# Turning score blocks three groups ahead instead of two, and mixing token groups in pairs, in a fused gated-attention and token-mixing kernel

## The chip, the cores and the metric

The kernel runs on one core of a Trainium2 chip. The metric is device time in microseconds (us); lower is better. Engines are called as in the profile: PE is TensorE's matmul side and PEld its weight load, DVE is VectorE, ACT is ScalarE, POOL is GpSimd, SP is SyncE, which here only issues transfers. A name with a q at its end (SPq, POOLq) is the engine's sequencer.

## The reference, cut to what matters

```python
# B, S, D = 8, 3200, 256; d_qk = d_hyper = 64; inputs and output are float32
scores = (1.0 / S) * np.matmul(z, z.transpose(0, 2, 1))     # symmetric: token by token
attn   = np.maximum(scores, 0.0) ** 2
x      = u * np.matmul(attn, v)
wq, wk = x @ w_q, x @ w_k
W_tok  = (1.0 / np.sqrt(64)) * np.einsum('bsd,btd->bst', wq, wk)
mixed  = np.einsum('bst,btd->bsd', W_tok, x)
out    = np.maximum(mixed, 0.0) @ w_out
```

Nothing in `W_tok` is nonlinear, so the kernel never makes it. It forms the 64 x 256 matrix "heads" = wk^T x of a batch, and then mixes: mixed = wq times heads.

## The kernel before, in words

**Tiling.** The 3200 tokens of a batch are 25 tiles of 128, taken in seven groups: six of 512 tokens and a last one (`LASTG`, group 6) of 128. A score tile is 128 key tokens by the 512 queries of one group. The attention matrix is symmetric, so a block that was computed for groups (gi, gj), gi < gj, can serve (gj, gi) when it is transposed. `is_turned` (L177) says for which pairs that is done: gj at most `FAR` = 2 groups further, or gj the last group. The transposing is a DMA from SP (L268) from the tile `at` to `tt1`, `tt2` (by the distance) or `ttl`, and `weights` (L272) picks the direct or the turned block. The profile calls all numbered buffers `tt`.

**Phases.** The text is one long loop, `while groups` (L601); every pass is called a phase here, counted by `k`. A phase scores six new tiles as three pairs (four tiles, when it also mixes), L211: the two matmuls of a pair use 64 rows each and lie in the two halves of the array. DVE or ACT takes a pair out of PSUM (`first_stage`, L230/L234, tile `g`), and one phase later POOL or ACT squares it (`second_stage`, L247/L249, tile `at`). Two phases after its scoring (`LAG`), a tile may be used by the second product (L289), 128x256 matmuls into `acc`; each group needs 25 tiles times four column blocks (25 times one for group 6). The loop spreads a group over `m` phases by when its own tiles will have been scored; rows that come from turned blocks fill up (`left`).

**After a group's last phase,** `gate` (L315) multiplies by `u` on DVE into `x_sb`, and SP turns it (L327). Phases later `keys_and_heads` projects it (L337; `wqk` gives 64 rows of q and 64 of k), ACT writes it to `qk` (L348, pool `pq` with nine buffers), SP turns that to `kx` (L353). When the next group is keyed, `double_keys_queries` copies q to the other 64 partitions by a DMA (L361) and the keys to the other half of `kx` on POOL (L362), so that `heads` (L368) comes out doubled; DVE adds it up (L381) and closes it into `hs` (L387). `mix` (L416) then does one group, both halves of the model width side by side, `mix_out` applies relu on ACT (L428), and `proj` (L441) with `proj_out` (L463/L468/L469) makes and stores the output. One `mix` and its `proj` share a phase.

**The transfers' order.** SP issues everything that is not a load of `v` or `z` in the order of the text, and waits in that order: a transpose whose `at` is not squared yet holds the load of `u` behind it. POOL issues the loads of `v` (L127) and `z` (L131) between its squarings. `group_begun` (L555) sets the phases in which loads are due: `load_u` of the next group one phase after a group has begun.

**The end.** After the loop the keys of the last group are not turned but replaced by a Gram matrix (`last_gram`, `last_heads`); what is left of batch 6 and all of batch 7 is mixed, projected and stored there.

Of the kernel before, what the change touches and what calls it, by code (L numbers as in the profile page):

```python
# [16 lines left out]
def kernel(  # L17
# [25 lines left out]
    FAR = 2  # L43
# [6 lines left out]
    NAT = 14  # L50
# [9 lines left out]
    pg = ctx.enter_context(tc.tile_pool(name="pg", bufs=8))  # L60
# [4 lines left out]
    pq = ctx.enter_context(tc.tile_pool(name="pq", bufs=9))  # L65
    prt = ctx.enter_context(tc.tile_pool(name="prt", bufs=3))
# [82 lines left out]
    wq32 = consts.tile([P, ND, dh], FP32, tag="wq32", name="wq32")  # L149
    wk32 = consts.tile([P, ND, dh], FP32, tag="wk32", name="wk32")  # L150
    wqk = consts.tile([P, ND, 2, dh], FP16, tag="wqk", name="wqk")
    wq2 = consts.tile([P, ND, 2, dh], FP16, tag="wq2", name="wq2")
    wk2 = consts.tile([P, ND, 2, dh], FP32, tag="wk2", name="wk2")
    wo = consts.tile([P, ND, D], FP16, tag="wo", name="wo")
    wo32 = {}

    def load_weights():
        wo32[0] = px.tile([P, ND, D], FP32, tag="x_sb", name="wo32")
        nc.sync.dma_start(out=wq32[:], in_=moe_w_q.rearrange("(c p) h -> p c h", p=P))
        nc.sync.dma_start(out=wk32[:], in_=moe_w_k.rearrange("(c p) h -> p c h", p=P))  # L160
        nc.sync.dma_start(out=wo32[0][:], in_=moe_w_out.rearrange("(c p) e -> p c e", p=P))

    def cast_weights():
        nc.gpsimd.tensor_copy(out=wqk[:, :, 0, :], in_=wq32[:])
        nc.gpsimd.tensor_copy(out=wqk[:, :, 1, :], in_=wk32[:])
        for half in range(2):
            nc.gpsimd.tensor_copy(out=wq2[:, :, half, :], in_=wq32[:])
            nc.gpsimd.tensor_copy(out=wk2[:, :, half, :], in_=wk32[:])
        nc.gpsimd.tensor_copy(out=wo[:], in_=wo32[0][:])
# [7 lines left out]
    def is_turned(gi, gj):  # L177
        return gi < gj and (gj <= gi + FAR or gj == LASTG)

# [7 lines left out]
    for b in range(B):  # L187
        for gi in range(NG):
            near = [t for t in range(NT) if is_turned(gi, group_of(t))]
            own = [  # L190
                t for t in range(NT) if t not in near and not is_turned(group_of(t), gi)
            ]
# [47 lines left out]
    def second_stage(p0, g, on_act):  # L240
        at = pat.tile([P, 2 * W], FP16, tag="at", name="at")
        at0 = 0
        for hs, w in pieces(p0):
            n = hs.stop - hs.start
            out = at[:, at0 : at0 + n * w].rearrange("p (n w) -> p n w", w=w)
            if on_act:
                nc.scalar.square(out=out, in_=g[:, hs, 0:w])  # L247
            else:
                nc.gpsimd.tensor_mul(out=out, in0=g[:, hs, 0:w], in1=g[:, hs, 0:w])  # L249
            at0 += n * w  # L250
        at0, blocks = 0, []
        for tile_ in tiles[p0 : p0 + 2]:
            b, gi, ti = tile_
            made[tile_] = (at, at0)
            gj = group_of(ti)
            if is_turned(gi, gj):
                blocks.append((b, gi, gj, ti - starts[gj] // P, 1, at0, at0 + widths[gi]))
            at0 += widths[gi]
        if len(blocks) == 2 and blocks[0][:3] == blocks[1][:3] and blocks[1][3] == blocks[0][3] + 1:
            blocks = [blocks[0][:4] + (2, blocks[0][5], blocks[1][6])]  # L260
        for b, gi, gj, n0, nn, c0, c1 in blocks:
            if (b, gi, gj) not in turned:
                kind, nr, bufs = ("l", 1, 8) if gj == LASTG else (gj - gi, 4, gj - gi + 2)
                turned[b, gi, gj] = ptt.tile(
                    [P, nr, 4, P], FP16, tag=f"tt{kind}", name=f"tt{kind}", bufs=bufs
                )
            out = turned[b, gi, gj][:].rearrange("p n j t -> p (n j) t")
            nc.sync.dma_start_transpose(out=out[:, 4 * n0 : 4 * (n0 + nn), :], in_=at[:, c0:c1])  # L268
# [55 lines left out]
    def turn_x(b, gi):  # L324
        nn = widths[gi] // P
        xTs[b, gi] = pxt.tile([P, 4, ND, P], FP16, tag="xT_sb", name="xT_sb")
# [18 lines left out]
    def projections_out(b, gi, out):  # L345
        gw = widths[gi]
        qks[b, gi] = pq.tile([P, W], FP16, tag="qk", name="qk")
        nc.scalar.copy(out=qks[b, gi][:, 0:gw], in_=out)  # L348

    def turn_keys(b, gi):  # L350
        gw = widths[gi]
        ks[b, gi] = pk.tile([P, 4, 2, dh], FP16, tag="kx", name="kx")
        nc.sync.dma_start_transpose(  # L353
            out=ks[b, gi][:, 0 : gw // P, :, :].rearrange("p n a h -> p n (a h)"),
# [3 lines left out]
    def double_keys_queries(b, gi):  # L358
        gw = widths[gi]
        nn = gw // P  # L360
        nc.sync.dma_start(out=qks[b, gi][dh:P, 0:gw], in_=qks[b, gi][0:dh, 0:gw])  # L361
        nc.gpsimd.tensor_copy(out=ks[b, gi][:, 0:nn, 0, :], in_=ks[b, gi][:, 0:nn, 1, :])  # L362

    def heads(b, gis, ps, stop=True):

        parts = [(gi, n) for gi in gis for n in range(widths[gi] // P)]
        for gi, n in parts:
            nc.tensor.matmul(  # L368
                out=ps[:, 1, 0:D],
                lhsT=ks[b, gi][:, n, :, :].rearrange("p a h -> p (a h)"),  # L370
# [5 lines left out]
    def heads_out(b, gis, ps):  # L376
        if gis[0] == 0:
            hacc[b] = psml.tile([P, D], FP32, tag="ha", name="ha")
            nc.vector.tensor_copy(out=hacc[b][:], in_=ps[:, 1, 0:D])
        elif gis[-1] < LASTG:  # L380
            nc.vector.tensor_add(out=hacc[b][:], in0=hacc[b][:], in1=ps[:, 1, 0:D])  # L381
        else:
            heads_done(b, ps[:, 1, 0:D])

    def heads_done(b, part):
        hss[b] = psml.tile([P, D], FP16, tag="hs", name="hs")
        nc.vector.tensor_add(out=hss[b][:], in0=hacc.pop(b)[:], in1=part)  # L387
# [13 lines left out]
    def last_heads(b, g32, ps):  # L401
        for cc in range(ND):
            nc.tensor.matmul(
                out=ps[:, 1, 0:D],
                lhsT=wk2[:, cc, :, :].rearrange("p t h -> p (t h)"),
                rhs=g32[:, ds(cc * D, D)],
                start=False,
# [3 lines left out]
    def mix(b, gi):  # L411
        gw = widths[gi]
        ps = ps_tile("mx")
        for db in range(ND):
            half = db * dh
            nc.tensor.matmul(  # L416
                out=ps[:, db, 0:gw],
                lhsT=hss[b][half : half + dh, ds(db * P, P)],
                rhs=qks[b, gi][half : half + dh, 0:gw],
# [5 lines left out]
    def mix_out(b, gi, ps):  # L425
        gw = widths[gi]
        rts[b, gi] = prt.tile([P, ND, W], FP16, tag="rt", name="rt")
        nc.scalar.activation(out=rts[b, gi][:, :, 0:gw], in_=ps[:, :, 0:gw], func=RELU)  # L428
# [50 lines left out]
    def side_mix(b, ps):  # L479
        for db in range(ND):  # L480
            nc.tensor.matmul(
                out=ps[:, 1, ds(D + db * P, P)],
                lhsT=hss[b][:, ds(db * P, P)],
# [5 lines left out]
    def side_mix_out(b, ps):  # L489
# [3 lines left out]
            func=RELU, scale=0.5,  # L493
# [19 lines left out]
    todo_mix, todo_between, at_phase, side = [], [], {}, []  # L513
# [14 lines left out]
    def keys_and_heads(b, gis):  # L528
# [3 lines left out]
        projections(b, gis[0], wqk, outs[0])  # L532
        aside = None
        if keyed:
            heads(*keyed[0], ps, stop=(len(gis) == 1 and not side))
            if len(gis) > 1:
                projections(b, gis[1], wqk, outs[1], start=False)
# [6 lines left out]
        if keyed:  # L544
            hb, hgis = keyed.pop(0)
            heads_out(hb, hgis, ps)
            if hgis[-1] == LASTG:
                todo_mix.extend((hb, i) for i in range(LASTG))
# [6 lines left out]
    def group_begun(k, b, gi):  # L555
# [4 lines left out]
        if gi == 0 and b + 1 < B:  # L560
# [4 lines left out]
            for i in range(5):  # L565
                due(k + later + 5 + 3 * i, lambda i=i: load_v(b + 1, 5 * i, 5))
# [19 lines left out]
    def mix_due(k):  # L586
        if len(groups) > NG:
            return todo_mix and k - mixed_at[0] >= 3
        return len(todo_mix) > 2 and k - mixed_at[0] >= 2 and not key_due(k)
# [11 lines left out]
    while groups:  # L601
# [5 lines left out]
        if mix_due(k):  # L607
            mb, mg = todo_mix.pop(0)
            mixed_at[0] = k
            mixing = (mb, mg, mix(mb, mg))  # L610
# [8 lines left out]
        if keying and keyed:  # L619
            for g_ in keyed[0][1]:  # L620
                double_keys_queries(keyed[0][0], g_)
        if mixing:
            mix_out(*mixing)
        staged = []
# [29 lines left out]
        if begins:  # L654
# [5 lines left out]
            if m == 4 and need > produced + (4 if mix_due(k + 1) else 6):  # L660
# [20 lines left out]
        if mixing:  # L681
            mb, mg, _ = mixing
# [3 lines left out]
        elif keying:  # L686
            extra = todo_between.pop(0)[1]
        cut = 10 if extra else 0
# [28 lines left out]
    for g_ in hgis:  # L717
        double_keys_queries(hb, g_)
    psh = ps_tile("hd")
    heads(hb, hgis, psh, stop=False)  # L720
# [4 lines left out]
    for mb, mg in todo_mix[:2]:  # L725
        mix_out(mb, mg, mix(mb, mg))
    last_heads(last, g32, psh)
    heads_done(last, psh[:, 1, 0:D])
    for mb, mg in todo_mix[2:]:
        mix_out(mb, mg, mix(mb, mg))  # L730
# [4 lines left out]
    for i, (mb, mg) in enumerate(todo_mix):  # L735
        if i == 0:
            store(mb, mg, [acc_tile(0, "fo0")[:], acc_tile(1, "fo1")[:]],
                  [(True, nc.sync, 2), (True, nc.sync, 2)])
        else:
            store(mb, mg)  # L740
    qs = [(LASTG - 1, ps_tile("qq")[:, 0, :]), (LASTG, acc_tile(0, "qq")[:, 0:P])]
    for gi, o in qs:
        projections(last, gi, wq2, o)
    for gi, o in qs:
        projections_out(last, gi, o)
    mix_out(last, 0, mix(last, 0))
    for gi in range(LASTG - 1):
        mix_out(last, gi + 1, mix(last, gi + 1))
        if gi == LASTG - 2:
            mix_out(last, LASTG, mix(last, LASTG))  # L750
        store(last, gi)
# [32 lines left out]
```

## Time and profile before

| what | value |
|---|---|
| median of 3 runs | 808.53 us (808.15 to 812.89) |
| the profiled execution: time, span | 807.18 us, 805.4 us |
| PE, PEld busy, share of the span | 98%, 73% |
| DVE, ACT, POOL busy | 61%, 59%, 60% |
| score matmuls (L211), matmuls into `acc` (L289) | 920, 5000 |
| transposes of score blocks issued by SP (`tt`, `ttl`) | 146, 48 |
| mean traffic of the DMA engines | 178 GB/s |

The span goes from the first to the last instruction of the program; 1.8 us of the execution's time lie around it. A group line of the profile reads: line, engine, operation, tile written <- tiles read, shapes, count | busy us, mean ns of one | idle time of the engine before it, and what ended it. The DMA share is the time of all packets over that of 16 engines.

### The profile page before, as it was taken

What the parts mean: (1) busy time and instruction counts of PE and PEld (TensorE: products, weight loads), DVE (VectorE), ACT (ScalarE), POOL (GpSimd) and SP (SyncE); (2) the same over time, 40 slices, a digit from 0 to 9 for tenths busy, and PEclk for the clock granted to TensorE, in tenths of its full rate; (3) what the DMA queues carried; (4) which work ended last, traced back from release to release, by engine and by line L of the source; (5) the groups of instructions that cost most, each with busy time, mean ns of one, the idle gap of its engine ahead of it and who ended that gap; (6) DMA issues with size and microseconds to landing.
All of it is one profiled execution on the core that took longest, in us unless ns stands there. A gap on an engine that the chain in (4) does not pass through costs nothing.

```text
span 805.4 us, 16696 instructions
## 1 busy us (share of the span) xinstructions
PE 788.8 (98%) x6778; PEld 584.9 (73%) x6778; DVE 493.1 (61%) x514; ACT 475.1 (59%) x526; POOL 485.2 (60%) x352
## 2 busy tenths in 40 slices
PE   7999999999999999999999999999999999999996
PEld 4777777777777777777777777777777767767774
DVE  5766666565665566755676556765666656655525
ACT  6655556556765556565675556656665565565534
POOL 7957676564666557755666466864676555655420
PEclk9999999999999999999999999999999999999999
DMA  7999899997989969998899979999999996867436
GB/s 175 149 198 192 141 176 181 212 190 134 216 148 208 200 152 194 176 208 186 175 157 211 198 157 178 188 206 175 184 197 157 182 217 143 159 148 183 116 98 246
DMA packets 330878, 143.20 MB, mean 178 GB/s; under 512 B 307441, under 2 KB 313137, under 8 KB 330801
## 3 DMA queue, kind: packets, MB, share of 16 engines
q1 hardware_dynamic: 302528, 125.90, 76.4%
q0 software_dynamic: 28128, 15.98, 17.7%
q8 instruction: 53, 0.87, 0.5%
q10 hardware_dynamic: 144, 0.26, 0.1%
q14 instruction: 25, 0.20, 0.1%
HBM read 59.38 MB, written 26.21 MB: 106 GB/s over the span
## 4 chain that ended last, share of the span: by engine, by line
PE 95%; issue 1%; POOL 1%; DMA 1%; DVE 1%; ACT 0%; SPq 0%; POOLq 0%; DVEq 0%
PE acc L289 69%; PE sc L211 13%; PE fo L441 5%; PE qk L368 3%; PE qk L337 3%; PE mx L416 2%; POOL at L249 1%; DMA z<-in_z_dram 1%; DMA xT_sb<-x_sb 0%; DVE x_sb L315 0%; DVE fo L463 0%; PE qk L499 0%; ACT qk L348 0%; SPq L95 0%; DVE g L234 0%
## 5 line engine op out<-in xcount | busy, mean ns | idle before, releaser
L249 POOL TENSOR_TENSOR at<-g 128x1024 f16<-128x1024 f32 (+2 forms) x234 | 430.3, 1853 | 222.2 <-DVE g L234 136.8
L234 DVE TENSOR_SCALAR g<-sc 128x1024 f32<-128x1024 f32 (+1 forms) x340 | 388.1, 1184 | 188.5 <-PE sc L211 188.1
L289 PE MATMUL acc<-v_sb,at 128*128 128x256 f16 x3656 | 446.8, 273 | 0.4 <-DVE x_sb L315 0.4
L289 PEld LDWEIGHTS <-at 128*128 128x128 f16 x3656 | 344.7, 98 | 108.0 <-issue 66.6
L230 ACT ACTIVATE g<-sc 128x1024 f32<-128x1024 f32 x128 | 131.2, 1025 | 199.6 <-PE sc L211 199.6
L247 ACT ACTIVATE at<-g 128x1024 f16<-128x1024 f32 (+2 forms) x234 | 236.9, 1029 | 0.6 <-DVE g L234 0.6
L289 PE MATMUL acc<-v_sb,tt 128*128 128x256 f16 x1152 | 149.1, 273 | 0.0
L211 PE MATMUL sc<-zT 64*128 64x512 f16 x920 | 129.7, 381 | 2.3 <-DVE hs L387 0.9
L289 PEld LDWEIGHTS <-tt 128*128 128x128 f16 x1152 | 112.5, 98 | 12.9
L315 DVE TENSOR_TENSOR x_sb<-acc,u_sb 128x512 f16<-128x512 f32 (+1 forms) x104 | 69.3, 668 | 66.8 <-PE acc L289 62.5
L428 ACT ACTIVATE rt<-mx 128x1024 f16<-128x1024 f32 (+1 forms) x49 | 49.1, 1012 | 56.8 <-PE mx L416 55.3
L211 PEld LDWEIGHTS <-zT 64*128 64x128 f16 x920 | 34.9, 95 | 50.1 <-issue 28.5
L362 POOL COPY kx<-kx 128x256 f16<-128x256 f16 (+1 forms) x54 | 20.1, 378 | 65.9 <-DMA kx<-qk 65.7
L468 ACT ACTIVATE fo<-fo 128x1024 f32<-128x1024 f32 (+1 forms) x40 | 40.6, 1014 | 24.4 <-PE fo L441 22.6
L441 PE MATMUL fo<-wo,rt 128*128 128x256 f16 x386 | 49.6, 273 | 1.7 <-DVE fo L463 0.9
L348 ACT CAST qk<-qk 128x512 f16<-128x512 f32 (+1 forms) x54 | 28.7, 545 | 27.5 <-PE qk L368 13.2
L441 PEld LDWEIGHTS <-rt 128*128 128x128 f16 x386 | 37.2, 98 | 7.5 <-ACT rt L428 1.9
L381 DVE TENSOR_TENSOR ha<-ha,qk 128x256 f32<-128x256 f32 x31 | 13.1, 421 | 30.0 <-ACT qk L348 30.0
L368 PE MATMUL qk<-x_sb,kx 128*128 128x256 f16 x191 | 28.4, 273 | 1.9 <-POOL kx L362 1.9
L337 PE MATMUL qk<-xT_sb,wqk 128*128 128x512 f16 (+1 forms) x108 | 29.9, 358 | 0.0
L368 PEld LDWEIGHTS <-kx 128*128 128x128 f16 x195 | 19.0, 98 | 14.2 <-POOL kx L362 2.4
L289 PE MATMUL acc<-v_sb,ttl 128*128 128x256 f16 x192 | 22.6, 273 | 0.0
(47 smaller groups left out, 150.2 us busy)
## 6 DMA issues: line engine op xcount, KB each, us to landing
u_sb<-in_u_dram SPq DMA_DIRECT2D x48, 512.0 KB, 4.8
out_dram<-fo SPq DMA_DIRECT2D x46, 512.0 KB, 4.2
v_sb<-in_v_dram POOLq DMA_DIRECT2D x35, 320.0 KB, 5.7
qk<-qk SPq DMA_DIRECT2D x47, 64.0 KB, 4.0
zd<-in_z_dram POOLq DMA_DIRECT2D x7, 400.0 KB, 8.1
tt<-at SPq DMA_TRANSPOSE x146, 4.3
u_sb<-in_u_dram SPq DMA_DIRECT2D x8, 128.0 KB, 3.0
xT_sb<-x_sb SPq DMA_TRANSPOSE x56, 4.1
```

What stands on the lines that cost most here:

```text
L211: nc.tensor.matmul(out=sc[:, h, 0:gw], lhsT=zT[b][half : half + dqk, ts(ti, P)], rhs=zT[b][half : half + dqk, ds(gs, gw)], start=True, sto ...
L230: nc.scalar.activation(out=g[:, hs, 0:w], in_=sc[:, hs, 0:w], func=RELU, scale=GSCALE)
L234: nc.vector.tensor_scalar(out=g[:, hs, 0:w], in0=sc[:, hs, 0:w], scalar1=0.0, scalar2=GSCALE, op0=AOP.max, op1=AOP.mult,)
L247: nc.scalar.square(out=out, in_=g[:, hs, 0:w])
L249: nc.gpsimd.tensor_mul(out=out, in0=g[:, hs, 0:w], in1=g[:, hs, 0:w])
L289: nc.tensor.matmul(out=accs[j // 2][:, ds((j % 2) * D, D)], lhsT=weights(b, gi, ti, j), rhs=vs[b][:, ti, :], start=(first and ti == rows_[ ...
L315: nc.vector.tensor_mul(out=xs[b, gi][:, 2 * half : 2 * half + n, :].rearrange("p n d -> p (n d)"), in0=accs[half][:, 0 : n * D], in1=us[b, ...
L337: nc.tensor.matmul(out=out, lhsT=w[:, ac, :, :].rearrange("p t h -> p (t h)"), rhs=xTs[b, gi][:, 0 : gw // P, ac, :], start=(start and ac ...
L368: nc.tensor.matmul(out=ps[:, 1, 0:D], lhsT=ks[b, gi][:, n, :, :].rearrange("p a h -> p (a h)"), rhs=xs[b, gi][:, n, :], start=((gi, n) == ...
L428: nc.scalar.activation(out=rts[b, gi][:, :, 0:gw], in_=ps[:, :, 0:gw], func=RELU)
L441: nc.tensor.matmul(out=banks[jf // 2][:, ds((j - jf) * D, D)], lhsT=rt[:, dc, ts(j, P)], rhs=wo[:, dc, :], start=(dc == 0 and j == jf), st ...
L468: nc.scalar.mul(out=flat_out[:, sl], in_=part, mul=FINAL_SCALE)
```

## The change

- **Turned blocks.** `is_turned` takes the batch too: three groups further for batches 0 to 6, two for the last. Buffers: three for each of the distances 1, 2 and 3 (distance 2 had four), seven for the last group (eight before).
- **Order of a group's tiles.** Rows that are turned for the next group come first, and the single tile 24 goes to the end or the start, so that pairs stay whole.
- **q of odd groups on the other half.** A second weight tile `wkq` has k first and q second. Odd groups and group 6 are projected with it. The DMA copy of q (L361) and the POOL copy of the keys (L362) are gone; `heads` keeps only the half that holds k^T x, even and odd groups apart, and `heads_crossed` adds the two halves once per batch.
- **Mixing in pairs.** One `mix` does two groups for one half of the model width, with one matmul in each half of the array; the projections of the two groups wait in a list `todo_proj` until both halves are mixed, and take one phase each.
- **Group 6** has small tiles of its own for turned x and for q; its side mix uses `hz`, whose first 64 rows are zero.
- **Pools.** `at` 13 (14), `g` 7 (8), `qk` 11 (9), `rt` 2 of double size (3).
- **Loads.** `load_v` starts two phases earlier in a batch (four in the first one).
- **The end.** Two half mixes of batch 6 and two of its projections are left for the end (before: three mixes and three projections); batch 7 is mixed in pairs there too, and one relu of its first pair goes to DVE.

```diff
-    def is_turned(gi, gj):
-        return gi < gj and (gj <= gi + FAR or gj == LASTG)
+    def is_turned(b, gi, gj):
+        far = 3 if b + 1 < B else 2
+        return gi < gj and (gj <= gi + far or gj == LASTG)
...
-            elif len(tiles) % 2:
-                order = own[:1] + near + own[1:]
             else:
-                order = near + own
+                single = [NT - 1]
+                order = [t for t in near if group_of(t) == gi + 1 < LASTG]
+                order += [t for t in own + near if t not in order + single]
+                order = single + order if len(tiles) % 2 else order + single
...
-                kind, nr, bufs = ("l", 1, 8) if gj == LASTG else (gj - gi, 4, gj - gi + 2)
+                kind, nr, bufs = ("l", 1, 7) if gj == LASTG else (gj - gi, 4, 3)
...
-    def double_keys_queries(b, gi):
-        gw = widths[gi]
-        nn = gw // P
-        nc.sync.dma_start(out=qks[b, gi][dh:P, 0:gw], in_=qks[b, gi][0:dh, 0:gw])
-        nc.gpsimd.tensor_copy(out=ks[b, gi][:, 0:nn, 0, :], in_=ks[b, gi][:, 0:nn, 1, :])
+    def swapped(gi):
+        return gi % 2 == 1 or gi == LASTG
...
     def heads_out(b, gis, ps):
+        mine = slice(0, dh) if swapped(gis[0]) else slice(dh, P)
...
+        acc, part = hacc[b][mine, :], ps[mine, 1, 0:D]
+        if gis[0] < 2:
+            nc.vector.tensor_copy(out=acc, in_=part)
         else:
+            nc.vector.tensor_add(out=acc, in0=acc, in1=part)
+
+    def heads_crossed(b):
+        hx = psml.tile([P, D], FP32, tag="hx", name="hx", bufs=1)
+        nc.vector.tensor_copy(out=hx[0:dh, :], in_=hacc[b][dh:P, :])
+        nc.vector.tensor_copy(out=hx[dh:P, :], in_=hacc[b][0:dh, :])
+        return hx
+
+    def heads_done(b):
+        hx = heads_crossed(b)
         hss[b] = psml.tile([P, D], FP16, tag="hs", name="hs")
+        nc.vector.tensor_add(out=hss[b][:], in0=hacc.pop(b)[:], in1=hx[:])
+        nc.vector.tensor_copy(out=hz[b % 2][dh:P, :], in_=hss[b][dh:P, :])
...
+    def mix(b, pair, db):
+        ps = ps_tile("mx")
+        for a in range(2):
+            half = a * dh
+            nc.tensor.matmul(
+                out=ps[:, a, :],
+                lhsT=hss[b][half : half + dh, ds(db * P, P)],
+                rhs=qks[b, 2 * pair + a][half : half + dh, :],
+                start=True,
+                stop=True,
+            )
+        return ps
...
             for i in range(5):
-                due(k + later + 5 + 3 * i, lambda i=i: load_v(b + 1, 5 * i, 5))
+                due(k + later // 2 + 3 + 3 * i, lambda i=i: load_v(b + 1, 5 * i, 5))
...
         if mixing:
             mix_out(*mixing)
+            if mixing[2] == 1:
+                todo_proj.extend((mixing[0], 2 * mixing[1] + a) for a in range(2))
...
-            if m == 4 and need > produced + (4 if mix_due(k + 1) else 6):
+            if m == 4 and need > produced + (4 if mix_due(k + 1) or todo_mix else 6):
...
-        if mixing:
-            mb, mg, _ = mixing
+        if mixing and todo_proj:
+            mb, mg = todo_proj.pop(0)
...
+        elif len(groups) <= NG and todo_proj and gi < LASTG:
+            mb, mg = todo_proj.pop(0)
```

More of the change, by code (lines that the diff above doesn't have):

```diff
@@ L188 @@
         for gi in range(NG):
-            near = [t for t in range(NT) if is_turned(gi, group_of(t))]
+            near = [t for t in range(NT) if is_turned(b, gi, group_of(t))]
             own = [
-                t for t in range(NT) if t not in near and not is_turned(group_of(t), gi)
+                t for t in range(NT) if t not in near and not is_turned(b, group_of(t), gi)
             ]
@@ L607 @@
         if mix_due(k):
[L608 removed]
+            mixing = todo_mix.pop(0)
             mixed_at[0] = k
[L610 removed]
+            mixing += (mix(*mixing),)
             n = 4
@@ L724, with mix_next @@
     nc.vector.tensor_copy(out=g32[:, D : 2 * D], in_=psg[:, D : 2 * D])
[L725 to L730, printed above, removed]
+    heads_out(hb, hgis, psh)
+    hx = heads_crossed(last)
+    nc.vector.tensor_add(out=hx[:], in0=hx[:], in1=hacc.pop(last)[:])
+    def mix_next():
+        mb, pair, db = todo_mix.pop(0)
+        mix_out(mb, pair, db, mix(mb, pair, db))
+        if db == 1:
+            todo_proj.extend((mb, 2 * pair + a) for a in range(2))
@@ L744 @@
[L744 to L751, printed above, removed]
+    for _ in range(min(2, len(todo_mix))):
+        mix_next()
+    last_heads(last, g32, psh)
+    hss[last] = psml.tile([P, D], FP16, tag="hs", name="hs")
+    nc.vector.tensor_add(out=hss[last][:], in0=hx[:], in1=psh[:, 0, 0:D])
@@ new lines @@
+    assert not todo_mix
+    store(*todo_proj.pop(0), [acc_tile(0, "fo0")[:], acc_tile(1, "fo1")[:]],
+          [(True, nc.sync, 2), (True, nc.sync, 2)])
+    mix_out(last, 0, 0, mix(last, 0, 0))
+    mix_out(last, 0, 1, mix(last, 0, 1), on_dve=True)
+    while todo_proj:
+        store(*todo_proj.pop(0))
+    qs = [(LASTG - 1, acc_tile(0, "qq")[:]), (LASTG, acc_tile(1, "qq")[:, 0:P])]
+    for pair in range(1, LASTG // 2):
+        for db in range(ND):
+            store(last, 2 * pair - 2 + db)
+            if pair == 1 and db == 0:
+                for gi, o in qs:
+                    projections(last, gi, wq2, o)
+                for gi, o in qs:
+                    projections_out(last, gi, o)
+            mix_out(last, pair, db, mix(last, pair, db))
@@ L752 @@
+    last_mix(last)
+    store(last, LASTG - 2)
     store(last, LASTG)
```

131 lines of the change are left out of this document (69 added, 62 removed).

## The prediction

> **What bounds the kernel now.** I read the page's busy times first, then its chain, then the timeline of PE, the waits, and last the transfers.
>
> ```profile
> PE 788.8 (98%) x6778; PEld 584.9 (73%) x6778; DVE 493.1 (61%) x514; ACT 475.1 (59%) x526; POOL 485.2 (60%) x352
> ...
> PE 95%; issue 1%; POOL 1%; DMA 1%; DVE 1%; ACT 0%; SPq 0%; POOLq 0%; DVEq 0%
> ```
>
> PE is in use for 98% of the span and holds 95% of the chain; the other engines have a third of their time free. Whether PE is full, and not only busy, shows in start times.
>
> ```profile
> 302.38 0.82 PE L211 MATMUL sc<-zT 64*128 64x512 f16 x6
> 303.14 2.79 PE L289 MATMUL acc<-v_sb,at 128*128 128x256 f16 x24
> 305.86 0.39 PE L416 MATMUL mx<-qk,hs 64*128 64x512 f16 x2
> 306.09 0.59 PE L211 MATMUL sc<-zT 64*128 64x512 f16 x4
> 306.62 1.27 PE L289 MATMUL acc<-v_sb,at 128*128 128x256 f16 x10
> 307.72 1.04 PE L441 MATMUL fo<-wo,rt 128*128 128x256 f16 x8
> 308.59 2.13 PE L289 MATMUL acc<-v_sb,at 128*128 128x256 f16 x18
> 310.65 0.82 PE L211 MATMUL sc<-zT 64*128 64x512 f16 x6
> ```
>
> From start to start there is no hole: 10 matmuls of 256 columns take 1.10 us, 8 projections 0.87, so 0.109 us each. Six score tiles take 0.76 (302.38 to 303.14), four 0.53, so 0.23 per pair. The 24 matmuls behind take 2.72, 0.10 more than 24 times 0.109: the switch to the next scores. A phase's scores thus cost 0.86 us with three pairs and 0.63 with two; the rest of a phase is 0.109 per matmul. So the time is the sum of what PE has to do, plus its few waits:
>
> ```profile
> PE qk L368 <- POOL kx L362: 1.9, 1, 1.9
> ...
> PE sc L211 <- DVE hs L387: 0.9, 1, 0.9
> ```
>
> The trace is one execution of 807.18 us with a span of 805.4; the median of the runs shown, 808.53, lies 1.35 above it. I count in the span and add both differences at the end.
>
> **Part 1, fewer scores.** Per batch, pairs of 512-token groups at most two apart number 5 + 4 = 9, at most three apart 12. Each saves 4 score tiles, so 12 tiles in each of 7 batches: 920 becomes 836. Walking the loop by its own rules (six tiles a phase, four when mixing, the sizes `m`) gives 170 phases before: 127 with three pairs, 39 with two, one with one, three with none. After: 156, with 112, 41, 0 and 3. PE: before 127 x 0.86 + 39 x 0.63 + 0.40 = 134.2 us, after 112 x 0.86 + 41 x 0.63 = 122.1. **-12.1 us.** The 5000 second-product matmuls stay; the turned ones are only read from `tt`. The 42 pairs less on DVE, ACT and POOL lie under PE and give nothing.
>
> **Part 2, more transposes.** The 12 tiles per batch go out as 6 transposes: 42 more on SP, 1.29 us each (below), 54 us of SP's time; the 54 copies of q (L361, 0.5 to 0.6 us in the timeline) go, about -30. SP works under PE, so nothing, while what it brings is early. PE's idle time before the matmuls that read `tt` is 0.0:
>
> ```profile
> L268 SPq DMA_TRANSPOSE tt<-at x146: 1217/1292/4685, 20.5 to 745.9; - x146
> ```
>
> ```profile
> L289 PE MATMUL acc<-v_sb,tt 128*128 128x256 f16 x1152 | 149.1, 273 | 0.0
> ```
>
> In the walk a turned block is read at least five phases after its scoring before; after, four last-group blocks (in batches 1, 3, 5 and 7) have three, some 15 us, against a phase until squaring, SP's queue and a landing of 8.5 at most. 0, bound 3 us for each of the four. `tt2` with three buffers: the fourth block of a batch, (3,5), takes that of (0,2), which group 2 has closed at least two phases earlier. `at`: at most 21 tiles wait at a phase's start and 13 pairs hold 26. `g`: six live and one is free. 0 for these.
>
> **Part 3, keys, q and heads.** POOL loses 54 copies (0.40 us) and, above all, its waits for the transposed keys:
>
> ```profile
> POOL kx L362 <- DMA kx<-qk: 65.7, 18, 8.6
> ```
>
> The longest, 8.6 us, is the one behind which `heads` stood for 1.9 us at 656 us; POOL's squarings queued behind it too, and SP's transposes behind those. The second hole, at 717 to 719, is 0.9 + 0.2 + 0.2 us: ACT's cast of q stood for a `qk` buffer until a mix had read it. After, each new `qk` tile takes a buffer whose mix was at least nine phases earlier (eleven instead of nine, and group 6 aside). **-3.2 us** for both; 0 if new holes of the kind come. The crossing adds per batch two half copies, an add and a small copy on DVE: none is in the trace; between 0 and the 0.42 us of the 128x256 rows each, under 1.7 us in a phase of 5, with DVE at 61%: 0; uncovered at most 12 us in all. The casts for `wkq` (0.3 us each) and two memsets, on POOL early on: 0.
>
> **Part 4, mixing in pairs.** Matmuls and relus number the same. One more mix (0.23) and projection (0.87) fall into the loop: **+1.1**, and leave the end. **The end** ran from 783.2 to 801.2 on DVE. PE has 1.1 less there, but both relus of a pair must be through before its first projection, DVE loses one 1.22 us scaling and gains a relu of that size and three small passes. Laying the rows one behind another by engine and buffer, I get the same 18 us: **0**, between -1.5 and +2.
>
> **Part 5, loads.** POOL issues 0.6 us of `v` and 1.6 of `z` in one phase now: 2.2 and up to 3.8 of squaring against 3.5 to 5 of PE, with a phase of slack: 0, at worst 1 us in six batches. For `u` I allow something. SP is late:
>
> ```profile
> 652.02 0.82 PE L211 MATMUL sc<-zT 64*128 64x512 f16 x6
> ...
> 659.09 0.57 SPq L146 DMA_DIRECT2D u_sb<-in_u_dram  x1
> ```
>
> This load belongs to the phase of 652.02 and is issued 7.1 us into it; over all loads the landing comes 1.3 to 16.2 us into the phase (two far earlier). In the walk, group 5 gets only two phases in batches 0, 4, 5 and 6 (never before), and then `u` of group 6 has from its phase's start to its gate 6.5 + 3.6 us and what is mixed or keyed between, 10 to 12. A late `u` holds the gate on DVE, behind it the next scores' eviction, and PE, which needs `acc`. Per place 0 to 6 us; with landings near 8 in the middle I take **+1** in sum.
>
> **The sum:** -12.1 - 3.2 + 1.1 + 0 + 1 = -13.2: a span of 792.2, an execution of 794.0, and with 1.35 to the median 795.3; I say **795.5 us**.
>
> **Two rules of the Trainium skill.** PE's row is 98%. The Trainium skill, Perfetto Trace Analysis, Identifying the Most-Contended Engine, calls matmul busy time a poor measure of headroom and wants the weight loads' share; that is 73% here, and by it a quarter of PE would be free. The start times above decide against it in this kernel; its result stands among the rivals.
>
> The DMA rows:
>
> ```profile
> q1 hardware_dynamic: 302528, 125.90, 76.4%
> q0 software_dynamic: 28128, 15.98, 17.7%
> ```
>
> ```profile
> 300.00:400.00 100.00, 100.00 (x867) 74.61 (x866) 62.52 (x65) 59.65 (x67) 63.65 (x44) 1.00 1.05 189
> ...
> 780.00:805.00 25.00, 17.79 (x139) 12.11 (x136) 12.46 (x15) 10.70 (x14) 0.00 (x0) 0.99 0.62 226
> ```
>
> The queues' packets fill 95% of 16 engines. But in the table of stages (last two columns: share and GB/s) one stretch has a share of 1.05, which no real occupancy can have, with PE full, and the last moves 226 GB/s at 0.62. The same section calls the occupancy of 16 DMA engines misleading; by that the transfers have room, by the share they have none, which is the next rival.
>
> **Rivals.** *DMA becomes the bound (slower).* q1 and q0 and the rest hold 94.7% of 805.4, 763 us. 42 transposes of 256 KB are 11.0 MB; at q1's 615 us for 125.9 MB that is 54, less 15 for 3.1 MB of q copies: 802 us of transfers, and with some 10 of start and end a span of 812. By packets (43,008 of 256 bytes more, at the queue's mean of 32.5 ns over 16 engines) it is 87 less 7: 843, a span of 853. It decides once the transfers need more than PE's 792. Taken between: 825 to 830 us. For it: the share. Against: the stretch at 1.05, and landings of 4 us that nobody awaits. The Trainium skill's DMA: Bandwidth & Descriptors, Specifications, asks 512 bytes or more per transfer for line rate, so it counts these packets as dear.
>
> *SP too late.* The four loads of `u` each late by 4 to 6 us, some of the four short blocks by 3, POOL's bunched loads: 16 to 24 us would eat the gain: 806 us. For it: landings at 12 to 16 us into a phase. Against: SP no longer waits for squarings that POOL held back for keys.
>
> *PE is not full.* Then fewer scores only widen its idle time, and the execution keeps its length or gains the 3.2: 806 us. Against it: the start times.
>
> **How the numbers follow.** Forecast 0.81; SP too late 0.11; PE not full 0.03; DMA bound 0.05. The forecast's own bounds: without the allowance and with a better end 792, with both holes back, a worse end and 3 us of late loads 803. With part of the SP rival the range is 790 to 804. A measurement tells about 1% (8.1 us) from no change: faster by more means under 800.4. That takes 0.81 less some 0.01, and 0.03 of the SP rival: 0.83. Slower by more (above 816.6) is the DMA rival: 0.05. Within: 0.12.
>
> **What would show it.** After: 836 score matmuls, 188 transposes into `tt`; PE's rows for `acc` 5000 as before at 0.109 apart; no wait on POOL `kx`; PE idle near 16 us or less in all; the end still some 18 us. Wrong: PE waiting at L289 for DVE `x_sb`, with that one waiting for `u`; PE waiting for `tt`; PE busy under 96%; or score phases that cost less than 0.86 us when taken away.

## The result and the profile after

The change makes the kernel slower: 867.34 us (861.43 to 873.22, median of 6 runs) against 808.78 us, a ratio of 1.0734 (95% interval 1.0693 to 1.0775). The forecast was 795.5. Times here are medians of all executions of a kernel; a ratio and its interval compare only the fast ones, those within 1.5% of the kernel's fastest, with those of the kernel before, so it is not exactly the ratio of two medians. The profiled execution took 870.04 us with a span of 868.2, which is 76.0 over the forecast span of 792.2.

The page after, in its lines on busy times, the granted clock, the queues and the chain:

```profile
PE 798.8 (92%) x6694; PEld 592.5 (68%) x6694; DVE 472.4 (54%) x516; ACT 441.4 (51%) x495; POOL 426.3 (49%) x279
...
PEclk9997999899999999899989999989897999999999
...
q1 hardware_dynamic: 342560, 133.71, 79.2%
q0 software_dynamic: 28128, 15.98, 17.5%
...
PE 82%; DMA 11%; SPq 2%; ACT 2%; DVE 1%; issue 1%; POOL 1%; ACTq 0%; POOLq 0%; DVEq 0%
```

PE has 84 instructions less and is still busy 10.0 us longer, and idle for 69.4 us where it was idle for 16.6. The chain names the new partner: DMA, 11% against 1%. Which transfer it is stands in the waits of PE (us in total, times, longest):

```profile
PE qk L383 <- DMA kx<-qk: 49.5, 12, 8.6
PE sc L220 <- DMA zT<-zd: 3.6, 1, 3.6
```

and in the groups, whose last column is the idle time before them:

```profile
L298 PE MATMUL acc<-v_sb,tt 128*128 128x256 f16 x1488 | 191.7, 278 | 0.0
...
L383 PE MATMUL qk<-x_sb,kx 128*128 128x256 f16 x191 | 32.6, 300 | 50.4 <-DMA kx<-qk 49.5
```

So the blocks that are turned three groups ahead are never waited for (0.0, now over 1488 matmuls). What PE waits for is `kx`, the transposed keys of `heads`, a tile that has nothing to do with the score blocks except that SP issues both in one order. The longest such place, in the timeline of PE:

```profile
659.09 0.59 PE L349 MATMUL qk<-xT_sb,wkq 128*128 128x512 f16 x2
668.31 1.03 PE L383 MATMUL qk<-x_sb,kx 128*128 128x256 f16 x4 [8.62 <-DMA kx<-qk]
669.13 0.42 PE L349 MATMUL qk<-xTl,wkq 128*128 128x128 f16 x2
669.35 4.53 PE L298 MATMUL acc<-v_sb,at 128*128 128x256 f16 x22
```

Two things are to be read here. PE stands for 8.62 us. And the 22 matmuls behind it take 4.53 us, 0.206 each, where such matmuls took 0.109 in the forecast's rows: after the wait PE runs at half its speed for some us, and the trace grants it half the clock from 663.1 to 673.4. Why the keys came late is in the timeline of SP for the same stretch:

```profile
644.22 6.77 SPq L277 DMA_TRANSPOSE tt<-at  x3
651.08 3.76 SPq L277 DMA_TRANSPOSE ttl<-at  x2
654.93 4.87 SPq L277 DMA_TRANSPOSE tt<-at  x1
659.90 2.40 SPq L368 DMA_TRANSPOSE kx<-qk  x1
662.39 5.70 SPq L277 DMA_TRANSPOSE tt<-at  x2
```

ACT had cast these keys by 649.80. They went out at 659.90, behind six transposes whose issue alone took 15.4 us, 2.6 each (a median of 1.3 over the kernel), and landed some 8 us later. In the middle of this POOL issued two loads:

```profile
648.73 1.60 POOL L130 DMA_DIRECT2D zd<-in_z_dram  x1
650.33 0.56 POOL L126 DMA_DIRECT2D v_sb<-in_v_dram  x1
```

In the kernel before they stood two phases apart:

```profile
595.18 1.60 POOL L131 DMA_DIRECT2D zd<-in_z_dram  x1
...
603.09 0.61 POOL L127 DMA_DIRECT2D v_sb<-in_v_dram  x1
```

Over the whole kernel the SP transposes that are issued while a POOL load is in flight take 2.31 us to issue and 6.9 to land (means), the others 1.44 and 3.7; before the change it was 1.97 and 5.8 against 1.46 and 3.4. Those into `tt` alone, which are of one kind, differ in the same way (2.37 and 7.0 against 1.51 and 4.2 after).

**The sum closes.** At full speed PE's work should have been busy for 788.8 - 11.0 = 777.8 us; it is busy for 798.8, so the lower clock costs 21.0 (the mean granted clock fell from 0.999 to 0.961; in `f1_d2_z_early` below, at 0.998, PE is busy for those 777.8). Idle should have been 16.6 - 3.2 = 13.4 and is 69.4: 56.0. Less the 1 us allowed for late loads, that is the 76.0. The stage table (granted clock, share and GB/s at the end of a line) shows that the loss is not spread evenly, but sits in stages:

```profile
600.00:700.00 100.00, 86.29 (x703) 63.19 (x700) 51.08 (x56) 44.78 (x51) 45.08 (x27) 0.91 1.00 170
700.00:800.00 100.00, 99.30 (x863) 74.94 (x862) 59.41 (x65) 60.05 (x69) 45.37 (x26) 1.00 0.85 179
```

The second of these has about as many packets (41,376 against 41,714) and SP transposes (43 against 41) and moves more bytes, but it has one POOL load where the first has five, and PE is full there.

### The profile page after: what moved, and what is told of

It reads as the page before. It is cut to its first block, busy times and chain, and to the rows that moved or that the text cites. A ratio compares the mean times of both kernels' runs of the same rounds, so it can differ in the third digit from the quotient of the medians.

```text
span 868.2 us, 16360 instructions
## 1 busy us (share of the span) xinstructions
PE 798.8 (92%) x6694; PEld 592.5 (68%) x6694; DVE 472.4 (54%) x516; ACT 441.4 (51%) x495; POOL 426.3 (49%) x279
## 4 chain that ended last, share of the span: by engine, by line
PE 82%; DMA 11%; SPq 2%; ACT 2%; DVE 1%; issue 1%; POOL 1%; ACTq 0%; POOLq 0%; DVEq 0%
PE acc L298 60%; PE sc L220 10%; DMA kx<-qk 9%; PE fo L489 5%; PE qk L383 3%; PE qk L349 2%; SPq L277 2%; PE mx L441 2%; DMA zT<-zd 1%; POOL at L258 1%; DMA kx<-ql 1%; ACT g L239 1%; ACT at L256 1%; DVE fo L511 1%; PE ztp L117 0%
## 5 line engine op out<-in xcount | busy, mean ns | idle before, releaser
L258 POOL TENSOR_TENSOR at<-g 128x1024 f16<-128x1024 f32 (+1 forms) x211 | 387.9, 1850 | 403.9 <-DVE g L243 246.6
L243 DVE TENSOR_SCALAR g<-sc 128x1024 f32<-128x1024 f32 (+1 forms) x310 | 357.6, 1196 | 190.5 <-PE sc L220 188.4
L298 PE MATMUL acc<-v_sb,at 128*128 128x256 f16 x3320 | 417.1, 278 | 0.0
L239 ACT ACTIVATE g<-sc 128x1024 f32<-128x1024 f32 (+1 forms) x116 | 115.0, 994 | 224.0 <-PE sc L220 223.9
L256 ACT ACTIVATE at<-g 128x1024 f16<-128x1024 f32 (+1 forms) x215 | 218.8, 1028 | 5.2 <-DMA tt<-at 4.3
L298 PE MATMUL acc<-v_sb,tt 128*128 128x256 f16 x1488 | 191.7, 278 | 0.0
L298 PEld LDWEIGHTS <-tt 128*128 128x128 f16 x1488 | 148.4, 100 | 19.7
L220 PE MATMUL sc<-zT 64*128 64x512 f16 (+1 forms) x836 | 118.0, 381 | 5.0 <-DMA zT<-zd 3.6
L462 ACT ACTIVATE rt<-mx 128x1024 f16<-128x1024 f32 x47 | 48.0, 1025 | 69.7 <-PE mx L441 69.7
L383 PE MATMUL qk<-x_sb,kx 128*128 128x256 f16 x191 | 32.6, 300 | 50.4 <-DMA kx<-qk 49.5
L363 ACT CAST qk<-qk 128x512 f16<-128x512 f32 x47 | 27.5, 586 | 82.1 <-PE qk L383 31.7
L489 PEld LDWEIGHTS <-rt 128*128 128x128 f16 x384 | 36.9, 98 | 8.3 <-issue 1.8
L397 DVE COPY ha<-qk 64x256 f32<-64x256 f32 x16 | 6.8, 423 | 36.9 <-ACT qk L363 36.9
```

The source lines that it names most:

```text
L220: nc.tensor.matmul(out=sc[:, h, 0:gw], lhsT=zT[b][half : half + dqk, ts(ti, P)], rhs=zT[b][half : half + dqk, ds(gs, gw)], start=True, sto ...
L239: nc.scalar.activation(out=g[:, hs, 0:w], in_=sc[:, hs, 0:w], func=RELU, scale=GSCALE)
L243: nc.vector.tensor_scalar(out=g[:, hs, 0:w], in0=sc[:, hs, 0:w], scalar1=0.0, scalar2=GSCALE, op0=AOP.max, op1=AOP.mult,)
L298: nc.tensor.matmul(out=accs[j // 2][:, ds((j % 2) * D, D)], lhsT=weights(b, gi, ti, j), rhs=vs[b][:, ti, :], start=(first and ti == rows_[ ...
L383: nc.tensor.matmul(out=ps[:, 1, 0:D], lhsT=ks[b, gi][:, n, :], rhs=xs[b, gi][:, n, :], start=((gi, n) == parts[0]), stop=(stop and (gi, n) ...
L462: nc.scalar.activation(out=out, in_=ps[:], func=RELU)
```

## The experiments

Two theories stood against each other. *Slack*: the keys' transposes always had little time to spare, and anything that delays SP's queue a little makes PE wait. *Ceiling*: the DMA engines can't move more, so the time follows the packets. A third, *SP's order*, was tried on the way: SP's issuing, not the transfers, is what is late. In the expectations S, D and Q stand for these three; T blames the added transposes, L the meeting of the loads of `z` and `v`, and P the changed keys. The edits are against the kernel after unless said otherwise. A wait inside the loop is tabulated from PE's start times, between 22 us after the start and 22 us before the end, as what a gap has over its usual length; "slow" is what consecutive `acc` matmuls have over 0.109 us. Both are of the one profiled execution; in the kernel before the granted clock never falls inside the loop, so its 3.6 is what "slow" counts without that. The ratio is to the kernel before. "Late" means as in the kernel before, but for the first batch, whose loads stay as early as the change put them.

| run | turned further | loads of `v` start | heads | ratio (95%) | waits, slow (us) |
|---|---|---|---|---|---|
| before | none | late | usual | 1 | 3.7, 3.6 |
| after | three groups | early | usual | 1.0734 (1.0693–1.0775) | 56.3, 18.8 |
| x1_loadv | three groups | late | usual | 1.0339 (1.0289–1.0390) | 31.6, 11.4 |
| x2_far2 | none | early | usual | 1.0239 (1.0187–1.0291) | 13.4, 8.8 |
| y1_far2_loadv | none | late | usual | 1.0047 (1.0020–1.0074) | 11.2, 5.8 |
| p03 | only (0,3) | late | usual | 1.0082 (1.0050–1.0114) | 10.7, 6.8 |
| d2_after | three groups | early | later | 1.0229 (1.0175–1.0284) | 28.0, 10.0 |
| d2_loadv | three groups | late | later | 1.0140 (1.0080–1.0200) | 17.4, 7.4 |
| f1_d2_z_early | three groups | late, behind `z` | later | 0.9998 (0.9962–1.0034) | 11.6, 5.3 |
| f2_d2_only03 | only (0,3) | late, behind `z` | later | 0.9956 (0.9930–0.9981) | 3.8, 5.0 |
| f3_d2_far2 | none | late, behind `z` | later | 1.0043 (1.0023–1.0064) | 5.1, 5.1 |

**The two parts undone, and one done alone.** `x1_loadv` puts the loads of `v` that are issued in batches 1 to 6 back to where they were, `x2_far2` turns two groups ahead as before, `x4_b_far3` does only the turning in the kernel before (with the change's buffers for `tt` and `ttl`).

```diff
# x1_loadv
-                due(k + later // 2 + 3 + 3 * i, lambda i=i: load_v(b + 1, 5 * i, 5))
+                due(k + 5 + 3 * i, lambda i=i: load_v(b + 1, 5 * i, 5))
# x2_far2
-        far = 3 if b + 1 < B else 2
+        far = 2
# x4_b_far3 (against before)
-        return gi < gj and (gj <= gi + FAR or gj == LASTG)
+        far = 3 if b + 1 < B else 2
+        return gi < gj and (gj <= gi + far or gj == LASTG)
```

> The changed kernel with the loads of v two phases later again (in the first batch they stay two later than before the change allows, five phases after the batch's begin). Theory T (the 42 added transposes of score blocks make SP's queue and the DMA engines late for the keys): hardly a change, 855 to 868 us, PE still waits some 40 us for the keys' transpose. Theory L (v's first load beside z's chokes the transfers, and the keys' transpose behind them is late): the waits in the keying of group 4 of every batch go, about half of the 50 us, and the slow clock behind them: 820 to 835 us.

> The changed kernel with blocks turned two groups further only, all else as changed. Theory T: the waits for the keys go, PE does 84 score tiles more: 800 to 812 us. Theory L: the z and v loads still meet, so waits of 20 us and more remain: 825 to 850 us. Theory P (the changed keys themselves, without the copy on POOL, are to blame): waits remain as they are, 870 to 880 us.

> The kernel before with blocks turned three groups further (all but the last batch), and nothing else of the change. Theory T: it is slow as the changed kernel, over 830 us, with PE waiting for the keys on POOL. Theory L and theory P: the gain of the score tiles shows, 795 to 800 us.

Measured: 835.94, 826.65 and 836.41 us; before took 806.55 in these runs, and `x4_b_far3` is at 1.0370 (1.0326 to 1.0414). By the ratios some 32 of the lost us hang on when `v` is loaded, and some 40 on the turning three groups ahead; the two overlap, for the whole loss is 59. No theory is enough alone: `x4_b_far3` falls where T put it, `x2_far2` where L did, `x1_loadv` at the upper edge of L's range, and P is out. The turning alone costs 30 us in the kernel before as well, where the forecast's Part 1 had it at -12. There the keys still go by POOL, and PE waits for that copy:

```profile
PE qk L369 <- POOL kx L363: 22.5, 9, 4.5
PE sc L212 <- DMA zT<-zd: 7.2, 1, 7.2
```

**The keying later in its phase.** `x3_late` moves the whole keying (the projection, `heads` of the group before, the cast and the transpose of the new keys) to four matmuls before the phase's end, and ACT's squarings ahead of it.

```diff
+        if keying:
+            cut = max(10, len(matmuls) - 4)
```

> The changed kernel with the keying put four matmuls before its phase's end instead of ten matmuls after its start. If the late keys are the cause of the loss, whatever makes them late, each of the dozen waits is 1 to 3 us shorter, and fewer reach the length behind which the clock falls: 825 to 850 us. If PE's waits only show where a general shortage of transfers ends, the time goes to other waits: 860 us and more.

Measured: 874.02 us, 1.0839 (1.0788 to 1.0890). The waits for keys fell to 30.8 us in 5 places, but others came for them (9.9 us for `zT` in one place); all of PE's waits sum to 65.7 us, against 63.4 after. The edit gives the keys no more time: their cast moves back together with the `heads` that use them, and from cast to `heads` it is 14.8 us in the median against 15.3 after. So it is no test of slack, and its expectation of shorter waits was not put to the test either; `d2_after` below is one, with 28.7 us.

**Both undone, and three looks at what holds SP up.** `y1_far2_loadv` joins the edits of x1 and x2. `y2_no_v` leaves the loads of `v` out from the second batch on. `y3_stores_act` is x1 with the loop's stores issued by ACT. `y4_z_whole` is x1 with `z` loaded in one piece into a tile of its own and copied twice by DVE.

```diff
# y2_no_v, in load_v
-        if n0 == 0:
-            vs[b] = pv.tile([P, NT, D], FP16, tag="v_sb", name="v_sb")
+        vs[b] = vs[0]
+        return
# y3_stores_act (and the same in side_proj_out)
-                proj_out(mb, mg, proj(mb, mg), [(False, nc.sync, widths[mg] // P)])
+                proj_out(mb, mg, proj(mb, mg), [(False, nc.scalar, widths[mg] // P)])
# y4_z_whole
+        nc.gpsimd.dma_start(out=zcs[b][:], in_=rows(z, b))
...
+        nc.vector.tensor_copy(out=zds[b][:, :, 0, :], in_=zc[:])
+        nc.vector.tensor_copy(out=zds[b][:, :, 1, :], in_=zc[:])
```

> The changed kernel with both undone: blocks turned two groups further only, and v's loads five phases after the batch's begin as before. If the added transposes and the meeting of the z and v loads are the whole cause, PE's waits for keys fall under 3 us, and what is left of the change gives what was forecast for it: 800 to 806 us. If the changed keys (no POOL copy, so the transposes are issued in another rhythm) or the tiles' order have a share, 812 to 822 us.

> The changed kernel without the loads of v of batches 1 to 7: every batch uses the v of batch 0. SP's queue is untouched; the DMA engines lose the larger part of the queue that takes 17.5% of them. Theory D (the 16 DMA engines have no room left, and hold SP's issues up): the waits for the keys all but go, 795 to 805 us. Theory Q (SP's own order: each issue 1.3 us, and waits for squarings in between): only the meeting with z goes, 830 to 840 us as with v loaded later.

> The changed kernel with v loaded as before the change, and with the output stores of the loop issued by ACT, behind ACT's own scaling, instead of by SP. The bytes are the same; SP loses some 50 issues and the waits before them (33 us). Theory Q: the waits for keys shrink clearly against the kernel with v loaded later, 805 to 820 us. Theory D: no change against it, 830 to 840 us.

> The changed kernel with v loaded as before the change, and with z loaded in one contiguous row per partition into a tile of its own, which DVE copies into both places (one buffer of at less for the room). 22,400 packets of 128 bytes, near 50 us of each DMA engine, become some hundred large ones; SP's queue has the same issues. Theory D: the waits shrink, 810 to 822 us. Theory Q: no change, 830 to 840 us.

Measured: 811.96 us (1.0047), 803.00 (0.9927, 0.9896 to 0.9959), 846.98 (1.0465, 1.0408 to 1.0522) and 841.81 (1.0423, 1.0362 to 1.0483). With both undone the loss is gone but for half a per cent. Without `v` the kernel with all its 188 transposes is faster than before, though q1 alone is at 83.5%:

```profile
PE qk L383 <- DMA kx<-qk: 3.7, 4, 2.0
```

So what the 42 transposes cost is set by what else is in flight; that fits the ceiling too, which had 795 to 805 here, and slack and ceiling are parted only by the runs below. SP's order alone is not the cause: `y2_no_v` leaves SP's queue as it is, and PE hardly waits. Nor are the stores in that queue: without them the waits for keys are no shorter (36.9 us against x1's 26.2). But the order has a share. From the end of a key's cast to the issue of its transpose it is 1.8 us before and 1.5 in `x2_far2`, 4.4 after and 4.5 in `y2_no_v` (medians): the added transposes in the queue put it off, with or without `v`. What `v` adds is the long cases: at most 20.1 us after, 12.8 in `y2_no_v`. The Trainium skill, Perfetto Trace Analysis, DMA Optimizations, says that balancing DMAs over the engines that issue them may help where descriptor generation is the bottleneck; here, done with the stores, it brought nothing. `y4_z_whole` is a miss: `z` came in 6.7 us instead of x1's 9.3 (medians), with 21,504 packets less on q0, and the time did not fall. It also has one `at` buffer less, so its own cost is not cleanly told.

**Slack given to the keys, and fewer bytes.** `d2_after` lets `heads` of batches 0 to 6 follow two keyings later instead of one, with a buffer more in `px` and `pk` and one less in `at`; `d2_loadv` adds x1. `n_u` loads one tile of `u` and uses it everywhere. `p03` is x1 with only the block pair (0,3) turned three groups ahead.

```diff
# d2_after
+        depth = 2 if len(groups) > NG else 1
+        while len(keyed) > depth:
+            ...
+        ready = len(keyed) == depth
...
-        if keyed:
+        if ready:
# n_u, in load_u
+        if u0:
+            us[b, gi] = u0[0]
+            return
# p03
-        return gi < gj and (gj <= gi + far or gj == LASTG)
+        return gi < gj and (gj <= gi + (far if gi == 0 else 2) or gj == LASTG)
```

> The changed kernel with the heads of a group taken two keyings after its keys were turned, not one (in batches 0 to 6; one more buffer each for turned keys and x, one less for at): the keys get some 15 us more. Theory S (there is room for all transfers in the mean, and bursts hit the keys because they have the least slack): the waits for keys go and with them the slow clock, what remains is a wait or two for turned z: 798 to 815 us. Theory D (the transposes and the loads together fill what the DMA engines can do): the waits move to turned z, turned score blocks or u: 840 us and more.

> The same with v loaded as before the change. Theory S: 790 to 800 us, the gain that was forecast. Theory D: 820 us and more.

> The changed kernel with u loaded once only and that tile used by all groups: 26 MB and 55 of SP's issues less, while POOL's loads stay. If bytes on the DMA engines are what is short, whichever queue brings them: 800 to 820 us, as without v. If it is POOL's queue of loads that holds up SP's transposes: 840 us and more.

> The changed kernel with v loaded as before the change, and of the blocks three groups apart only (0,3) turned: 14 transposes more than with two groups, not 42. If the loss grows with the number of transposes: a third of the way from 812 to 836 us, 818 to 822. If it needs a full queue to begin, 806 to 812, as the 28 score tiles less save 4 us of PE.

Measured: 827.06, 820.89, 816.89 (1.0087, 1.0052 to 1.0122) and 814.76 us. With the same transfers and two keyings of time no key is waited for any more (each lands at least 3.2 us before its `heads`); what is left of PE's waits in `d2_after` is another late transfer, `z` of the second batch, which is turned two phases before its first use in this version:

```profile
PE sc L220 <- DMA zT<-zd: 14.2, 1, 14.2
PE acc L298 <- DVE x_sb L324: 10.0, 8, 2.6
```

In time `d2_loadv` came out where the ceiling had it (820 and more), but its longest wait is this same `z` (11.3 us), not a key.

`n_u` shows that loads on SP's own queue count as well: 16.0 us of waits for keys instead of 49.5. It takes 55 issues out of that queue together with 25.7 MB, and does not tell which of the two counts. `p03` came out between its two expectations.

**The causes taken out together.** `f1_d2_z_early` is `d2_loadv` with `z` of the second batch loaded and turned two phases earlier, and the loads of `v` behind it there too. `f2_d2_only03` turns only (0,3) further in it, `f3_d2_far2` nothing.

```diff
# f1_d2_z_early, besides the edit of d2_after
-            later = 4 if b == 0 else 0
+            later = 2 if b == 0 else 0
...
-                due(k + later // 2 + 3 + 3 * i, lambda i=i: load_v(b + 1, 5 * i, 5))
+                due(k + later // 2 + 5 + 3 * i, lambda i=i: load_v(b + 1, 5 * i, 5))
```

> Heads two keyings later, v as before the change, and in the first batch z loaded, doubled and turned two phases earlier and v one phase later. Theory S (enough room, too little slack): 792 to 802 us, PE idle under 10 us between start and end. Theory D (too little room): another wait takes the place, 812 us and more.

> The same with only the blocks (0,3) turned three groups further: 14 transposes more than with two groups, 28 score tiles less. Theory S: some 8 us slower than f1, as PE has 56 score tiles more: 800 to 808 us. Theory D: faster than f1, 800 to 806 against 812 or more.

> The same with blocks turned two groups further only, so none of the 42 transposes: PE's sum is that of the kernel before, less its two holes. Theory S and theory D: 803 to 808 us; under S this is the slowest of the three, under D the fastest or level with f2.

Measured: 806.76 us (800.15 to 812.60), 803.00 and 810.51. `f1_d2_z_early` has every transfer of the change and is as fast as the kernel before. Its page:

```profile
PE 777.8 (97%) x6694; PEld 583.7 (73%) x6694; DVE 477.1 (59%) x516; ACT 439.7 (55%) x493; POOL 429.9 (53%) x281
...
q1 hardware_dynamic: 342560, 133.71, 83.6%
q0 software_dynamic: 28128, 15.98, 17.7%
```

Same packets as after, in a span of 803.6 us. Together with the three small queues (0.6%) their shares make 101.9%, so packet time is no occupancy and no limit at the 843 us of the forecast's rival: the ceiling falls in its plain form. But the time came out between what slack and ceiling had expected, and its executions scatter by 12 us: the slack there is thin too. PE is idle for 25.8 us, where the forecast had 14.4. Of that 6.7 us are behind DVE's `x_sb`, most of it for a late `u`: the longest wait, 3.5 us up to 468.91, stands behind a `u` that SP issued at 464.08 and that landed at 468.08. With the keys out of the way the late `u` of the forecast does show. `f2_d2_only03` is the version that beats both kernels, 0.9956 (0.9930 to 0.9981), a gain of 0.4% that the interval tells from nothing (from `f1_d2_z_early` it is not told apart: the intervals overlap; `f3_d2_far2` is the slowest of the three, as slack had it), with no wait for a transfer inside the loop:

```profile
PE acc L298 <- POOL at L258: 2.4, 1, 2.4
PE acc L298 <- DVE x_sb L324: 1.2, 2, 0.9
```

## Why the prediction was wrong, point by point

- **Part 1, fewer scores, and Part 4's +1.1: right.** 836 score matmuls, 5000 into `acc`, 0.109 us apart in the median. PE busy in `f1_d2_z_early` is 777.8, 11.0 below before, which is -12.1 + 1.1; that it fits to the tenth is luck, since "slow" differs by 1.7 us between the two. The score phases cost what was said; the gain was given back.
- **Part 2, more transposes at nothing: the step that failed.** The slack was taken from the blocks that are turned, which indeed are never waited for. It had to be taken from the tightest thing in the same queue. In the trace before, the time from the landing of a `kx` to its `heads` was already short: 0.5 us at the least, several tiles below 3, 6.8 in the median. The cast-to-heads time hardly grew (14.0 to 15.3 us in the median); what grew is the longest landing, 7.4 to 11.2 us, and the issues ahead of it: the longest time from cast to issue went from 10.2 to 20.1 us. Turning costs 30 us (`x4_b_far3`) to some 40 (`x2_far2`) even with the 12.1 that the scores save, so the term that was put at 0 is some 42 to 52.
- **Part 3, keys: the row was read from the wrong side.** "POOL kx <- DMA kx: 65.7, 18, 8.6" was booked as POOL's trouble, which would go with the copy. It said that keys come late 18 times. With the copy gone PE itself waits for them: 49.5 us, 12 times. The other hole, ACT's cast behind a `qk` buffer, is gone as forecast. The crossing was put at 0; PE waits 0.7 us for `hs` after it, and in `f3_d2_far2` once 2.4.
- **Part 5, loads: failed as well.** The issue of `z` and `v` in one phase was priced by POOL's time (0, at worst 1 us in six batches). What it changes is the flight: `z` lands in 13.0 us (median) instead of 8.1, `v` in 6.5 instead of 5.7, and the transposes beside them are slower. Putting `v` back is worth some 32 us. The late `u` was looked for in the wrong place: DVE waits for it once, 2.8 us.
- **The walk missed one batch.** Blocks had their five phases, but `z` of the second batch is turned two phases before its first use after the change, four before. That is one wait of 3.6 us in the kernel after, and of 14.2 in `d2_after`.
- **The end: right.** From the last `acc` matmul to the end of the span 22.3 us before, 22.4 after.
- **What a wait costs beside itself was missing.** For 56 us of idle time there are 21 more of slower work. The Trainium skill, Perfetto Trace Analysis, Matmul Optimizations, says that the matmul engine scales its power with its use and that matmuls should run back to back; the row of 0.206 us each behind an 8.62 us wait agrees.
- **The rival *SP too late* had the right queue and the wrong waiters.** It priced late `u` and late short blocks at 16 to 24 us. PE's idle time before matmuls that read `tt` or `ttl` is 0.0 after, and `u` held DVE for 2.8 us. Of the forecast's signs of being wrong only PE busy under 96% came (92%); a wait for `kx` was not among them.
- **The rival *DMA becomes the bound* was right in kind and given 0.05.** What spoke for it, a share of 95%, was set aside for the stretch at 1.05. That stretch shows that the share is no measure of occupancy; it does not show that there is room. Its price by packets, a span of 853, came near the 868.2, but by another mechanism: no ceiling, since `f1_d2_z_early` ends at 803.6 with the same packets.

**What stays open.** How much of the long issues (up to 5.8 us for one transpose of a score block) comes from the DMA engines being taken and how much from the path that transposes use; a transpose is in flight for 784 of 868 us after, and for 697 of 805 before, so either would fit; in `f1_d2_z_early` it is 741 of 804, a larger share than after, so that share alone sets no limit either. Why the quicker `z` of `y4_z_whole` brought nothing. And why `f3_d2_far2`, without further turning, is still 0.4% slower than before: its profiled execution has 0.9 us more of PE's work and 2.1 more of idle time, with one wait of 2.4 us for `hs` behind the crossing, but that is one execution.

## What to carry to other kernels

Price work that is added to an in-order queue by the least slack of anything else in that queue, not by the slack of the work itself; the first place to look is who already waits for that queue, even if it is an engine off the path. When the main engine is full, its waits cost more than their length, here by over a third (21 us on 56), because the clock falls. Find the slack first and spend it then: the same transfers cost 7.3% with one keying of slack and bunched loads, and nothing with two and the loads spread.

## What was not expected of the hardware

- After waits of several us PE works at half its speed for some us: 22 matmuls of 256 columns at 0.206 us each, against 0.109. In the kernel after, that follows every wait for keys of 3.09 us or more, and one of 1.94 with another of 0.90 right behind it; single waits of 1.30, 1.35 and 1.70 us are followed by full speed.
- A transpose on SP takes 1.44 us to issue and 3.7 to land with no load from POOL in flight, 2.31 and 6.9 beside one (means after the change). Leaving out 11.5 MB of loads of `v`, of 151 MB in all, gave back some 64 us.
